# Filter rows in half transfers and a smaller fetch constant in the schedule: attention beside a long convolution on one core

## The chip, the cores and the metric

One core of a Trainium2 chip runs the whole program. The metric is device time in microseconds from launch to end; the time given for a kernel is the median of its runs. The engines named here are TensorE (PE, with its weight loads as PEld), VectorE (DVE), ScalarE (ACT), GpSimd (POOL) and SyncE (SP). Data move through 16 DMA engines, which serve several queues.

## The reference

Two independent blocks share the output, each 2048 x 512: multi-head attention with 32 heads of 16 columns (A), and a long convolution of 512 channels with gates (B). All inputs are bfloat16.

```python
def _A_ref(x, wqkv, wo):                       # x (1, 2048, 512), H = 32, Dh = 16
    q, k, v = split(x @ wqkv)
    scores = jnp.einsum("bhqd,bhkd->bhqk", q, k) * (Dh ** -0.5)
    p = softmax(scores)
    o = jnp.einsum("bhqk,bhkd->bhqd", p, v)
    return merge_heads(o) @ wo

def _B_ref(q, k, v, shift_k, ssm_k, ssm_D):    # each channel alone, over 2048 positions
    k_shift = 4-tap causal filter of k with shift_k
    kv = k_shift * v
    y = causal convolution of kv with ssm_k (2048 taps, by FFT of length 4096)
    y = y + kv * ssm_D
    return q * y

return jnp.concatenate([a, b], axis=-1)
```

## The kernel before

**Attention.** The scores are cut into 2048 blocks of 128 keys by 512 queries. For a step, `qk_mm` (L728) writes the scores of two or three blocks into PSUM banks, `emit_exp` takes the exponential of most of them in one ScalarE instruction (L761, with 512 columns for each block) and, where it can, gives one block to VectorE, which works out the exponential in four operations (`exp_on_dve`: L803, L810 twice, L815). Two steps later `emit_pv` (L844) multiplies the results with the values into another bank. After 64 blocks a head group is closed: a transpose (L905), a reciprocal and a product (L912, L916), and after two groups a second transpose (L925). Projections of queries, keys and values are done in pieces between the steps: a bank is lent for a few steps (a window, opened in `take_banks` when a job is due within OPEN steps), and `unit_step` puts the pieces into it; SLOT says how many steps a job is reckoned to need.

**Convolution.** For each channel the filter, reversed and padded, lies in HBM as a row of `kz_scratch`. A Toeplitz tile is read from it by one DMA with overlapping rows: partition p gets the 2048 values that begin at p, so 128 rows of 4 KB, 512 KB. Four channels make a quad (`qd`), and 128 quads make the 512 channels. `load_wr` (L990 to L997) issues the four DMAs of a quad on SP's queue as soon as one of four quad-sized places in `WR` is free; `conv_lags` (L1003 to L1033) multiplies for a range of lags, each lag with four matmuls (L1014), one for each channel, side by side in the array. A quad has 16 lags, so 64 matmuls, and the whole convolution 8192. After each four quads the result goes to SBUF (L1028), and after eight quads it is turned by eight transposes (L1039, `conv_turn`) and multiplied with the gate (L1048).

**The order.** The program is written out in full ahead of time, by a planner that runs while the kernel is built. It has a clock for each engine (class `Eng`), and `done` holds the planned end of each operation and transfer. `dma` plans a transfer: it begins when its engine and its inputs allow, lands `late` (4.2 us) later at the earliest, and the transfers follow one another at DMA_KB (394 KB/us). The class `Tensor` also follows TensorE's instruction fetch: every matmul counts as two instruction words, a block is BLOCK (256) words, and when one block is used up the next must have landed; the one after it is then planned to land FETCH later:

```python
            cross = self.t - (1.0 - part) * min(kw.get("run", 0.0), self.t - t0)
            stall = max(self.lands - cross, 0.0)
...
            self.lands = cross + stall + FETCH
```

`spare` tells how many words may still be used without running into that landing. Between the steps of the attention, `emit_bg` puts in a burst of lags. Its size is the least of LAGS, a budget that grows with time by PACE (and is set so that the convolution ends END steps before the PLAN of 710 steps), the time that is left before ScalarE needs its next scores, and what `spare` allows:

```python
        left_us = max(1.14 * (PLAN - END - T), 1.0)
        st["lags"] = min(st["lags"] + min(PACE * st["left"] / left_us, RATE) * (pe.t - st["t"]), CAP)
...
        left = min(LAGS, int(st["lags"]), int((room(T) - pe.turn("C") - SWITCH) / LAG), int(pe.spare() / 8))
        while left > 0 and st["qd"] < wr_next[0] and kv_n[st["qd"] // 32] == 4 and at(h_wr[st["qd"]]) + WAIT <= pe.t:
```

So a quad is begun only when its transfers are planned to have landed 1.5 us (WAIT) before. Where TensorE would be idle, `warm_up` puts in small matmuls on zeros (L1219). `dve_block` (L775 on) decides whether a step gives a block to VectorE: the step needs three banks, no lent bank that stands in the way, little enough planned work on VectorE, and enough blocks left, a limit into which TAIL_GAP enters. TURN says by how much `conv_turn` may make the next scores late.

Every engine then runs its list in order; waits are semaphores. What TensorE really waits for at run time is set by the chip and not by the plan.

Of the kernel before, what the change touches and what calls it, by code (L numbers as in the profile page):

```python
# [11 lines left out]
S = 2048  # L12
# [15 lines left out]
LEFT = 16  # L28
LKR = LEFT + S
R_W = 16  # L30
R_PT = 18
R_Q = 3
R_A = 4
# [1 line left out]
PVB = 6  # L35
BGB = 7
N_OPEN = 66
LAGS = 7
PACE = 1.4
KEYS0 = 256  # L40
END = 8

# [14 lines left out]
R_EH = 2  # L59
R_PTD = 5  # L60
T_DVE = 6
SLOT = 16
OPEN = 80
CLOSE = 12
REST = 2
LEN = 3
# [9 lines left out]
Q_DUE = 24  # L76
LOOK = 8
GAP = 7
TAIL_GAP = 4
AHEAD = 4  # L80
KZ_LATE = 8.0
KEEP = 4
# [3 lines left out]
DMA_KB = 394  # L86
X_KB = 200
WINDOW = 3.4
HALF = 0.25
TURN = 0.2  # L90
SOON = 0.5
NEAR = 0.2
FULL = 1.6
# [11 lines left out]
LAG = 0.0555  # L105
BLOCK = 256
WORD0 = 62
FETCH = 6.3
NEED = 10.0
FILL = 0.054  # L110

# [50 lines left out]
class Calls:  # L162
# [8 lines left out]
    transpose = matmul  # L171


class Tensor(Eng):
# [7 lines left out]
    def op(self, fn, deps=(), **kw):  # L182
# [6 lines left out]
        if words >= self.left:  # L189
# [3 lines left out]
            if stall:  # L193
                self.stalls.append((cross, stall))
                self.t += stall
                if kw.get("inc", True):
                    self.done[(id(self.sem), self.n)] += stall
            self.lands = cross + stall + FETCH
        self.at_word += words
# [20 lines left out]
def bass_concat_heads__mha_block__ssm_conv_h3__prompt_kernel(  # L220
# [13 lines left out]
    kz_ap = nc.dram_tensor("kz_scratch", (C, LKZ), BF16).ap()  # L234
# [7 lines left out]
    def sem(name):  # L242
        return enter(nc.semaphore(name))

    def sb(name, shape, dt=BF16):
        return enter(nc.sbuf_tensor(name, shape, dt))
# [6 lines left out]
    QS = sb("QS", [128, QB])  # L253
    PT = sb("PT", [128, R_PT, QB])
    WR = sb("WR", [128, R_W, S])
    WRF = WR[:, :, :].rearrange("p r w -> p (r w)")
# [25 lines left out]
    VST = [x.rearrange("p (t d) -> p t d", t=NB)  # L282
           for x in (WR[:, R_W - 2, :], WR[:, R_W - 1, :], OUTA[:, :, :].rearrange("p r d -> p (r d)"), VS2[:, :])]
    KZS = WRF[:, 0:4 * LKZ].rearrange("p (c m) -> p c m", c=4)
# [13 lines left out]
    act, dve, pool, sp = [Eng(sem(n), done) for n in ("s_act", "s_dve", "s_pool", "s_sp")]  # L298
    dma_t = [0.0]

    def at(*deps):
        return pe.at(deps)

    def dma(eng, dsem, outp, inp, deps=(), transpose=False, kb=512, rate=DMA_KB, late=4.2):
        h = dsem.add()
        start = max(eng.t, at(*deps))
        dma_t[0] = max(dma_t[0], start + late) + kb / rate
        done[(id(h[0]), h[1])] = dma_t[0]

        def fn(e):  # L310
            f = e.dma_start_transpose if transpose else e.dma_start
            f(outp, inp).then_inc(dsem.sem, 16)  # L312
        issue = kb / (rate if rate < DMA_KB else 155) if transpose else 0.55
        eng.op(fn, deps, inc=False, us=(issue, issue + 0.06))
        return h

# [37 lines left out]
    d_outA = [DmaSem(sem(f"d_outA{i}")) for i in range(R_A)]  # L354
    d_wr = [DmaSem(sem(f"d_wr{i}")) for i in range(R_W // 4)]

# [24 lines left out]
    for c in range(4):  # L381
        src = bass.AP(tensor=v2.tensor, offset=v2[128 * (NB - 1), 128 * c].offset, ap=[[D, 128], [-128 * D, NB], [1, 128]])
        h_vn.append(dma(sp, d_kv[3 + c], VST[c], src, kb=512))

    def load_kt(i, dep):
        h_kt[i] = dma(sp, d_kv[i], KTR[i][:, :, LEFT:LEFT + S], k2[:, (0, 256, 384)[i]:(256, 384, 512)[i]], [dep], transpose=True, kb=(1024, 512, 512)[i])
        h_kt0[i] = pool.op(lambda e: e.memset(KTR[i][:, :, 0:LEFT], 0.0), [dep])
# [102 lines left out]
    def evac_unit(u, bank, h):  # L490
# [18 lines left out]
        elif kind == "kv":  # L509
# [6 lines left out]
            if sum(kv_n[0:2]) == 8 and c < 2:  # L516
                load_qn(0, [h])
                wr_free.append((R_W // 4 - 1, hh))
                load_wr()
# [15 lines left out]
    h_kzw = [None]  # L535
# [15 lines left out]
    def kz_store(us):  # L551
# [3 lines left out]
        load_kt(2, h_kzt[0])  # L555
        wr_free.extend([(i, h_kzw[0]) for i in range(R_W // 4 - 1)])
        load_wr()
# [55 lines left out]
    def take_banks(T):  # L613
# [24 lines left out]
        else:  # L638
# [3 lines left out]
            banks = list(range(ends[1], 6))  # L642
        if T >= N_OPEN and near(T, OPEN) and T >= win.get("last", 0) + REST and "bank" not in win and len(banks) > 2 and late["bank"] is None and len(queue) > LAST_BLKS + 18:
            b = hold(T, banks, "w")
# [4 lines left out]
    def near(T, most):  # L649
        job = next_unit(T)  # L650
        return job is not None and job[0] - T <= most

    def hold(T, banks, kind):
        if T % 2 == 0:
            b = banks.pop()
            ends[0] -= 1
        else:
            b = banks.pop(0)
            ends[1] += 1
        held[b] = kind  # L660
        h_held[b] = T
        return b
# [3 lines left out]
    late = {"bank": None}  # L666
# [75 lines left out]
    def emit_exp(T, bl, banks, h, extra, d_bank, more):  # L742
        n = len(banks)
        if extra is not None:
            on_dve[extra] = len(on_dve)
            exp_on_dve(extra, d_bank, h)
        if pt_at[0] + n > R_PT:
            pt_at[0] = 0
# [22 lines left out]
    def pt_next():  # L771
        p = pt_at[0]
        return set(range(p, min(p + MOST, R_PT))) | (set(range(MOST)) if p + MOST > R_PT else set())

    def dve_block(T, bl):  # L775
        if len(bl) < 3 or WIN_D and "bank" in win and (part[0] or WIN_D > 1 and near(T, CLOSE)) or T < T_DVE or len(queue) < LAST_BLKS + 3 * (TAIL_GAP - N_LAST) + 3:
            return None
        i = len(on_dve)
        if i >= R_FX and i - R_FX not in h_last:
            return None  # L780
        todo = sum(us[0] for f in flow for _, _, _, us, _ in f)
        if max(dve.t - pe.t, 0.0) + todo > BACKLOG:
            return None
        n = blk_group(bl[-1])
        if len([b for b in queue if blk_group(b) == n]) - 3 >= 2.6 * GAP:
            return bl[-1]
        n += 1
        ahead = [b for b in queue if blk_group(b) == n]
        if len(ahead) < 4 * KT - AHEAD + 1 or n not in h_q or (OF[n], 0) not in h_k:
            return None  # L790
        rows = [blk(b)[2] for b in bl[:-1]]
        return next((b for b in ahead[:4] if blk(b)[2] not in rows), ahead[0])
# [4 lines left out]
    def exp_on_dve(b, bank, h):  # L797
        i = on_dve[b]
        fx = FX[:, i % R_FX, :]
        frac = fx.bitcast(U16).rearrange("p (n w) -> p n w", w=2)[:, :, 0]  # L800
        eh = EH[:, i % R_EH, :]
        out16 = PTD[:, i % R_PTD, :].bitcast(U16)
        h_f = urgent(lambda e: e.tensor_scalar(fx, PS[:, bank, :], FIX_ADD, FIX_HI, ALU.add, ALU.min),  # L803
                     [h, h_last.get(i - R_FX)], slack=S_FX)
        bank_free[bank] = h_f
        st = {"h": h_f}

        def square(j, us):
            src = frac if j == 0 else eh
            st["h"] = dve.op(lambda e: e.scalar_tensor_tensor(eh, src, (P1, P2)[j], src, ALU.add, ALU.mult),  # L810
                             [st["h"], h_last.get(i - R_EH)], us=us)

        def last(us):
            h_last[i] = h_blk[b] = dve.op(
                lambda e: e.scalar_tensor_tensor(out16, eh, P3, fx, ALU.mult, ALU.add),  # L815
                [st["h"], h_ptd.get(i - R_PTD)], us=us)
        dep = lambda: [st["h"]]
        flow.append([("p", dep, lambda us: square(0, us), V512,
                      lambda: i < R_EH or i - R_EH in h_last),
                     ("p", dep, lambda us: square(1, us), V512, lambda: True),  # L820
                     ("p", dep, last, V512, lambda: i < R_PTD or i - R_PTD in h_ptd)])
# [162 lines left out]
    h_wr, h_qn = {}, {}  # L984
# [5 lines left out]
    def load_wr():  # L990
        while wr_free and wr_next[0] < C // 4:
            (i, dep), qd = wr_free.pop(0), wr_next[0]
            wr_next[0] += 1
            wr_slot[qd] = i
            for c in range(4):
                src = bass.AP(tensor=kz_ap.tensor, offset=kz_ap[4 * qd + c, 0].offset, ap=[[1, 128], [1, S]])
                h_wr[qd] = dma(sp, d_wr[i], WR[:, 4 * i + c, :], src, [h_kzw[0], dep])  # L997

    def load_qn(i, deps):
        h_qn[i] = dma(pool, d_q[0], QN[:, :, :],  # L1000
                      q2[:, 256 * i:256 * i + 256].rearrange("(t p) d -> p t d", p=128), deps, kb=1860)
# [71 lines left out]
    def room(T):  # L1073
        lim = at(h_exp[min(T, end[0] - 1)]) - 0.47 - MARGIN
        return lim - max(pe.t, at(bank_free[BGB]))
# [8 lines left out]
    def press(T):  # L1084
        load = max([(i + 1) * SLOT / max(due - T, 1) for i, (due, u) in enumerate(jobs)], default=0.0)
        return SOON if load > FULL else NEAR if load > 0.75 * FULL else 0.0

    def unit_step(T):
# [7 lines left out]
        while not tight:  # L1096
# [16 lines left out]
            else:  # L1113
                ahead = (due - win["begin"] - 5) / SLOT
                over = TURN if u[0] == "turn" else 9.0 if ahead <= 1 else press(T)
                if T == stop - 1 and ahead > 2 and u[0] != "turn":
# [26 lines left out]
    def emit_bg(T):  # L1143
# [20 lines left out]
        if not st["started"]:  # L1164
            return
        left_us = max(1.14 * (PLAN - END - T), 1.0)
        st["lags"] = min(st["lags"] + min(PACE * st["left"] / left_us, RATE) * (pe.t - st["t"]), CAP)
        st["t"] = pe.t
        left = min(LAGS, int(st["lags"]), int((room(T) - pe.turn("C") - SWITCH) / LAG), int(pe.spare() / 8))
        while left > 0 and st["qd"] < wr_next[0] and kv_n[st["qd"] // 32] == 4 and at(h_wr[st["qd"]]) + WAIT <= pe.t:  # L1170
# [146 lines left out]
```

## Time and profile before

| | us |
|---|---|
| median of 3 runs (lowest, highest) | 827.02 (825.85, 828.55) |
| the profiled execution | 828.52 |
| its span, first to last instruction | 826.8 |
| granted TensorE clock in it, mean | 0.996 |
| PE idle before matmuls of L728 | 38.7 |
| last exponential ends | 819.7 |
| packet records: q1 packets of 4096 B | 65536, 0.159 each |

The span is what lies between the first and the last instruction of the profiled execution, and the 1.7 us more in its own time lie around it; that execution was 1.5 us over the median. Busy times of an engine are unions of its instructions, so mean durations times counts can come out higher: neighbouring instructions overlap. q1 is the hardware queue that carries the transfers issued by SP, and q8 carries instruction blocks; a packet record has its queue, start, duration and size. A line of the chain is start, duration and what it was; a line of a timeline is start, duration, engine, line, operation, tiles, count, and in brackets the idle time before it with what ended it.

The stages, from the table of windows (columns: window, its length, then busy time and instructions of PE, PEld, DVE, ACT, POOL, then the granted clock, the busy share of the DMA engines and GB/s):

```profile
40.00:100.00 60.00, 56.23 (x686) 24.96 (x690) 60.00 (x103) 59.68 (x53) 5.04 (x9) 1.00 0.76 251
100.00:200.00 100.00, 92.60 (x1858) 41.84 (x1857) 98.45 (x169) 99.41 (x91) 11.45 (x24) 1.00 1.02 389
200.00:300.00 100.00, 91.50 (x1778) 38.60 (x1784) 96.28 (x166) 96.84 (x86) 7.62 (x16) 0.98 1.03 399
...
700.00:800.00 100.00, 90.61 (x1686) 37.24 (x1689) 96.58 (x166) 97.44 (x87) 4.11 (x8) 0.98 0.90 341
800.00:827.00 27.00, 21.00 (x207) 7.08 (x206) 17.30 (x32) 20.79 (x20) 1.18 (x1) 1.00 0.20 59
```

The first score exponential starts at 7.9 us, the lags run from 89.5 to 804.1, and from 100 to 790 us the DMA engines are busy nearly all the time.

### The profile page before, as it was taken

To read this page: it belongs to the slowest core of one execution; us is meant where nothing else is said; L and a number is where in the kernel's file an instruction comes from. 1 tells how busy PE (TensorE), PEld (TensorE's weight loads), DVE (VectorE), ACT (ScalarE), POOL (GpSimd) and SP (SyncE) were. 2 spreads that over 40 slices of the span, in tenths; PEclk is the share of its full clock that TensorE was granted. 3 is DMA by queue.
4 is the path that set the end of the run, shared out by engine and by line. 5 is a ranking of instruction groups with operands and counts; after the bars stand their busy time and mean duration, and the time that the engine had idled before them with its cause. 6 is when DMAs were issued, how large, how long until landed. Compare 5 with 4: busy or idle time off the path is not lost.

```text
span 826.8 us, 30549 instructions
## 1 busy us (share of the span) xinstructions
PE 762.2 (92%) x13603; PEld 324.2 (39%) x13642; DVE 794.2 (96%) x1360; ACT 807.0 (98%) x727; POOL 78.7 (10%) x155
## 2 busy tenths in 40 slices
PE   8998989999999899999899999999999999998987
PEld 3343434443333344444333344444433333333332
DVE  4999999999999899999999999999999999999985
ACT  6999999999999899999999999999999999999987
POOL 3300320010100101001011010101002002010000
PEclk9999999999999999999999999999999999999999
DMA  9998499999999999999999899999999999999922
GB/s 220 233 300 304 151 382 404 385 379 407 393 407 405 394 401 389 405 354 367 394 388 391 318 372 383 394 408 387 408 407 352 378 393 362 399 382 367 375 83 77
DMA packets 109235, 291.41 MB, mean 352 GB/s; under 512 B 37680, under 2 KB 41648, under 8 KB 108720
## 3 DMA queue, kind: packets, MB, share of 16 engines
q1 hardware_dynamic: 102256, 280.80, 90.8%
q0 software_dynamic: 5648, 8.27, 3.1%
q8 instruction: 108, 1.77, 0.9%
q10 hardware_dynamic: 1200, 0.39, 0.2%
q14 instruction: 23, 0.19, 0.1%
HBM read 276.83 MB, written 6.42 MB: 343 GB/s over the span
## 4 chain that ended last, share of the span: by engine, by line
ACT 77%; DVE 10%; PE 9%; issue 2%; DMA 1%; SPq 0%
ACT PT L761 77%; DVE EH L810 4%; PE PS L728 3%; DVE FX L803 2%; PE PS L1014 2%; PE PS L844 2%; DVE PTD L815 2%; PE PS L1219 1%; PE PS L468 1%; DMA xT<-in_A_x_dram 1%; DVE DT L905 0%; DVE YB L1028 0%; SPq L312 0%; DVE KV L514 0%; DVE OTN L925 0%
## 5 line engine op out<-in xcount | busy, mean ns | idle before, releaser
L761 ACT ACTIVATE PT<-PS 128x1024 bf16<-128x1024 f32 (+2 forms) x722 | 804.1, 1376 | 8.8 <-PE PS L728 8.3
L728 PE MATMUL PS<-QT,KTo 32*128 32x512 bf16 x2048 | 287.1, 385 | 38.7 <-ACT PT L761 14.1
L844 PE MATMUL PS<-PT,VA 128*32 128x512 bf16 x1771 | 199.7, 391 | 6.6 <-issue 3.5
L1014 PE MATMUL PS<-WR,KV 128*12 128x128 bf16 (+15 forms) x8192 | 201.6, 220 | 4.4 <-issue 4.3
L803 DVE TENSOR_SCALAR FX<-PS 128x512 f32<-128x512 f32 x277 | 187.9, 682 | 8.3 <-PE PS L728 8.0
L815 DVE SCALAR_TENSOR_TENSOR PTD<-EH,FX 128x512 uint16<-128x512 f32 x277 | 185.7, 677 | 0.0
L810 DVE SCALAR_TENSOR_TENSOR EH<-EH 128x512 f32<-128x512 f32 x277 | 185.4, 680 | 0.0
L810 DVE SCALAR_TENSOR_TENSOR EH<-FX 128x512 f32<-128x512 uint16 x277 | 184.5, 682 | 0.1
L1014 PEld LDWEIGHTS PS<-WR,KV 128*12 128x12 bf16 (+15 forms) x8192 | 140.6, 88 | 71.9 <-issue 42.5
L728 PEld LDWEIGHTS PS<-QT,KTo 32*128 32x128 bf16 x2048 | 73.3, 91 | 237.8 <-ACT PT L761 178.9
L1219 PE MATMUL PS<-IDN,ZW 128*32 128x512 bf16 (+3 forms) x498 | 132.2, 334 | 0.0
L312 POOL DMA_DIRECT2D QT<-QS x120 | 59.2, 501 | 483.7 <-DVE DR L912 133.7
L844 PEld LDWEIGHTS PS<-PT,VA 128*32 128x32 bf16 x1771 | 48.0, 93 | 114.0 <-issue 97.5
L844 PE MATMUL PS<-PTD,VA 128*32 128x512 bf16 x277 | 83.1, 383 | 0.0
L1219 PEld LDWEIGHTS PS<-IDN,ZW 128*32 128x32 bf16 x498 | 41.8, 96 | 24.1 <-issue 10.4
L905 DVE STREAM_TRANSPOSE DT<-PS 128x512 f32<-128x512 f32 x32 | 22.7, 709 | 7.3 <-PE PS L844 6.8
L1028 DVE CAST YB<-PS 128x512 bf16<-128x512 f32 x32 | 21.9, 684 | 1.4 <-PE PS L1219 1.1
L844 PEld LDWEIGHTS PS<-PTD,VA 128*32 128x32 bf16 x277 | 20.4, 95 | 1.6 <-DVE PTD L815 0.2
L955 PE MATMUL PS<-WKV,OTN 128*128 128x512 bf16 x53 | 16.9, 383 | 2.1 <-issue 1.6
L479 PE MATMUL PS<-WKV,xT 128*128 128x128 bf16 x256 | 18.1, 220 | 0.1
L456 PE MATMUL PS<-xT,WKV 128*128 128x512 bf16 (+1 forms) x52 | 15.0, 373 | 2.9 <-issue 1.1
L447 PE MATMUL PS<-xT,WQ 128*128 128x512 bf16 x45 | 14.4, 382 | 2.4 <-issue 2.1
(65 smaller groups left out, 209.2 us busy)
## 6 DMA issues: line engine op xcount, KB each, us to landing
WR<-kz_scratch SPq DMA_DIRECT2D x512, 512.0 KB, 8.4
kz_scratch<-WR SPq DMA_DIRECT2D x1, 2176.0 KB, 8.3
QN<-in_B_q_dram POOLq DMA_DIRECT2D x2, 1024.0 KB, 12.4
out_dram<-QN POOLq DMA_DIRECT2D x2, 1024.0 KB, 8.6
QT<-QS POOLq DMA_DIRECT2D x120, 16.0 KB, 5.3
out_dram<-OUTA POOLq DMA_DIRECT2D x12, 128.0 KB, 5.2
QN<-in_B_ssm_k_dram SPq DMA_DIRECT2D x1, 1024.0 KB, 8.3
OTN<-in_B_ssm_k_dram SPq DMA_DIRECT2D x1, 1024.0 KB, 9.2
```

Source lines behind the costliest of these rows:

```text
L312: f(outp, inp).then_inc(dsem.sem, 16)
L479: ins = e.matmul(PS[:, bank, 128 * j:128 * j + 128], lhsT=xT[:, dc, (4 * sc + j) * 128:(4 * sc + j + 1) * 128], rhs=WV[:, dc, o * 128:(o + ...
L728: ins = e.matmul(PS[:, bank, :], lhsT=KTo[32 * s:32 * s + 32, OF[n_] % 2, kt * 128:(kt + 1) * 128], rhs=QT[32 * s:32 * s + 32, n_ // 2 % R ...
L761: h_exp[T] = act.op(lambda e: e.activation(PT[:, p0:p0 + n, :].rearrange("p b f -> p (b f)"), PS[:, banks[0]:banks[0] + n, :].rearrange("p ...
L803: h_f = urgent(lambda e: e.tensor_scalar(fx, PS[:, bank, :], FIX_ADD, FIX_HI, ALU.add, ALU.min), [h, h_last.get(i - R_FX)], slack=S_FX)
L810: st["h"] = dve.op(lambda e: e.scalar_tensor_tensor(eh, src, (P1, P2)[j], src, ALU.add, ALU.mult), [st["h"], h_last.get(i - R_EH)], us=us)
L815: lambda e: e.scalar_tensor_tensor(out16, eh, P3, fx, ALU.mult, ALU.add),
L844: ins = e.matmul(dst, lhsT=w, rhs=rhs, start=(k == 0), stop=(k == KT - 1), tile_position=(0, 32 * s))
L905: h_t = urgent(lambda e: e.transpose(out=dt, in_=PS[:, PVB, :]), [h, h_mul.get(n - 1)], slack=S_T, us=(0.63, 0.751))
L1014: ins = e.matmul(PS[32 * c:32 * c + NB - n, BGB, 128 * (kk % 4):128 * (kk % 4) + 128], lhsT=KV[:, qd, n:NB, c], rhs=WR[:, r + c, 128 * (NB ...
L1028: hh = urgent(lambda e: e.tensor_copy(YB[:, half, :].rearrange("p (k i) -> p k i", k=4), src), [h, h_yb[0]], slack=S_C, us=V512)
L1219: pe.op(lambda e, s=s, k=k, rhs=rhs, bank=bank, rows=rows, c0=c0, first=first: e.matmul(PS[32 * s:32 * s + rows, bank, c0:c0 + 128 * k], l ...
```

## The change

The 128 rows of a channel's Toeplitz tile are loaded by two DMAs of 64 rows each: partitions 0 to 63, then 64 to 127, on the same queue and with the same semaphore, so a quad has eight DMAs and not four. The planner is told of 256 KB for each and of 0.42 us for its issue (0.55 before). FETCH goes from 6.3 to 5.4. Seven other constants of the planner change with it: LAGS, PACE, END, SLOT, OPEN, TAIL_GAP and TURN. What is computed stays the same; where each instruction stands is worked out anew.

```diff
+WR_P = 64
...
-LAGS = 7
-PACE = 1.4
+LAGS = 6
+PACE = 1.2
 KEYS0 = 256
-END = 8
+END = 16
...
-SLOT = 16
-OPEN = 80
+SLOT = 18
+OPEN = 100
...
-TAIL_GAP = 4
+TAIL_GAP = 3
...
-TURN = 0.2
+TURN = 0.05
...
-FETCH = 6.3
+FETCH = 5.4
...
-    def dma(eng, dsem, outp, inp, deps=(), transpose=False, kb=512, rate=DMA_KB, late=4.2):
+    def dma(eng, dsem, outp, inp, deps=(), transpose=False, kb=512, rate=DMA_KB, late=4.2, issue=0.55):
...
-        issue = kb / (rate if rate < DMA_KB else 155) if transpose else 0.55
+        issue = kb / (rate if rate < DMA_KB else 155) if transpose else issue
...
             for c in range(4):
-                src = bass.AP(tensor=kz_ap.tensor, offset=kz_ap[4 * qd + c, 0].offset, ap=[[1, 128], [1, S]])
-                h_wr[qd] = dma(sp, d_wr[i], WR[:, 4 * i + c, :], src, [h_kzw[0], dep])
+                for p in range(0, 128, WR_P):
+                    src = bass.AP(tensor=kz_ap.tensor, offset=kz_ap[4 * qd + c, p].offset, ap=[[1, WR_P], [1, S]])
+                    h_wr[qd] = dma(sp, d_wr[i], WR[p:p + WR_P, 4 * i + c, :], src, [h_kzw[0], dep], kb=4 * WR_P, issue=0.42)
```

## The prediction

> **What bounds the kernel now.** I read the busy table first, then the chain that ended last, then the costliest groups, then timelines around ScalarE's idle moments, and last the packet records of the DMA queues.
>
> ```profile
> PE 762.2 (92%) x13603; PEld 324.2 (39%) x13642; DVE 794.2 (96%) x1360; ACT 807.0 (98%) x727; POOL 78.7 (10%) x155
> ...
> q1 hardware_dynamic: 102256, 280.80, 90.8%
> ...
> q8 instruction: 108, 1.77, 0.9%
> ...
> ACT 77%; DVE 10%; PE 9%; issue 2%; DMA 1%; SPq 0%
> ...
> L761 ACT ACTIVATE PT<-PS 128x1024 bf16<-128x1024 f32 (+2 forms) x722 | 804.1, 1376 | 8.8 <-PE PS L728 8.3
> L803 DVE TENSOR_SCALAR FX<-PS 128x512 f32<-128x512 f32 x277 | 187.9, 682 | 8.3 <-PE PS L728 8.0
> ...
> WR<-kz_scratch SPq DMA_DIRECT2D x512, 512.0 KB, 8.4
> ```
>
> ScalarE is the bound: 804.1 of 826.8 us go to the 722 exponentials of L761 (1771 score blocks; the other 277 go to VectorE, L803 to L815). Only what ends its idle time, or moves blocks to VectorE, can shorten the span. Before the last block (818.7 us) ScalarE loses 8.8 us, 8.3 of them to scores that come late (L728). The longer pieces of the chain say why:
>
> ```profile
> 105.01 1.13 issue
> ...
> 222.63 1.19 issue
> 229.25 0.72 issue
> ...
> 354.97 0.99 issue
> ...
> 787.25 1.98 issue
> ```
>
> "issue" is TensorE waiting for nothing that the profile shows. A sixth such stop, 1.57 us, is in the timeline at 278.4:
>
> ```profile
> 278.27 0.09 PEld L728 LDWEIGHTS PS<-QT,KTo 32*128 32x128 bf16 x1 [0.28 <-DVE FX L803]
> ...
> 279.93 0.09 PEld L728 LDWEIGHTS PS<-QT,KTo 32*128 32x128 bf16 x2 [1.57 <-issue]
> ...
> 280.37 1.45 ACT L761 ACTIVATE PT<-PS 128x1536 bf16<-128x1536 f32 x1 [0.87 <-PE PS L728]
> ```
>
> One score operation is cut after its first of three weight loads, so no semaphore holds it. Queue q8 holds the reason: its 108 packets are 16 KB each, about 256 TensorE instructions. In all six stops TensorE resumes 1.3 to 1.6 us after such a packet landed. ScalarE's idle moments behind the six are 0.42, 0.46, 0.62, 0.87, 0.58 and 2.13 us; the two longest stops are followed by a granted clock of 0.5 for 3.4 us (from 281.2 and 789.8), with 1.13, 0.25 and 0.18 us more. Sum: **6.64 us** of the 8.8 are instruction fetch; TensorE stood still 7.58 us for it.
>
> **What a fetch costs now.** After the four middle stops (222 to 356 us) packet records give a whole cycle: from resuming to the start of the next packet 3.75 to 4.23 us (median 3.9), the packet 1.08, landing to resuming 1.3 to 1.6: 6.2 to 6.9 us. Packets are 6.0 to 6.4 apart in 27 of 107 intervals, closer in 10. So the schedule's 6.3 is about the usual cost and leaves nothing for a long one. One stop differs: after 789.23 the next packet started in 1.81 us, when only the last filter transfers (landed by 792.0) were still in flight. That cycle is 1.81+0.93+1.42 = 4.2 us.
>
> **The change part by part.**
> (1) Halved transfers. A 4 KB row takes a DMA engine 159 ns (median of 65536). A 128-row transfer is 8 rows on each of 16 engines, 1.27 us; the half is 0.64. The 2.1 us that loaded traffic adds to a fetch (3.9-1.8) are 1.65 such turns. If a fetch waits for whole transfers, halves take 1.05 us off: cycle 5.3. Ends: 4.2 (all the waiting goes) and 6.3 (the wait goes by bytes). I take 5.3, as 1.65 turns is what waiting behind a transfer under way and one behind it would look like.
> The Trainium skill, "DMA: Bandwidth & Descriptors", section "Queues, rings and completion order", says that each engine goes round its queues by packets, groups of typically 9 to 17 descriptors. If a group ends with its transfer the cycle is 5.3, else 6.3; no row here shows the groups.
> (2) Issues. 512 more on SP at 433 ns (median): a quad of four channels takes 3.46 us of SP instead of 1.73. Quads land at least 5.1 us apart (2 MB), so SP keeps up; a median of 6 transfers is in flight at an issue. With that cover gone (at most one in flight at 7 of 512 issues), the last half starts 1.7 us later, against a median of 6.3 us from a quad's landing to its first use (least 0.2). Nothing queues behind these on SP until the final stores. Cost 0; at worst one wait of 1.5.
> (3) 8192 more completion writes at 9 ns (median of the 4-byte packets), over 16 engines: 4.6 us each, or 0.036 on the 5.1 of a quad. Landings run from 101.7 (fifth quad) to 792.0, 690 us for 123 intervals that need 627: 63 us of slack hide it. END 8 to 16 asks for the convolution 8 steps earlier, about 9 us, so transfers could slow by (63-9)/627 = 8.6% before they set the end. Cost 0.
> (4) FETCH 5.4, LAGS 6, PACE 1.2. Same 8192 matmuls in L1014, in bursts of at most 24, not 28 (the burst before 278.4 has 28, and so 56 instructions). Bursts of 7 need 293 groups, of 6 need 341; at twice the 0.105 us that the code's SWITCH allows for a change of kind, 10 us of TensorE, hidden in its 64.6 idle us; uncovered it would be 10 us. The fetch limit stands 0.1 above my cycle where it stood at or under it. The six stops should mostly go. Ends: none goes (0), all go (-6.6). I take 60%: **-4.0 us**, as the longest cycles lie 0.6 above the usual one and some will still overrun.
> (5) VectorE idles 9.9 us between 100 and 800, 7.3 of it at these stops. An operation there starts every 0.60 us, a block takes four, 2.4 us: three blocks would fit. A block off ScalarE saves about 0.45 (two-block exponentials start every 0.91). TAIL_GAP 3 allows one more; VectorE is idle 6.25 us before 820.2, so it is in time. SLOT, OPEN and TURN move when a bank is lent to projections; a step with two banks cannot give VectorE a block. Ends: +3 blocks, -3 blocks, 1.35 us each way. I take one more: **-0.4**.
> Sum -4.4 on a profiled execution of 828.5 (span 826.8 and 1.7 around it) gives 824.1. The median of the runs is 827.0, 1.5 lower, so I forecast **822.6**.
>
> **Rivals.**
> *Fetch does not shorten* (slower side). The wait goes by bytes, the cycle stays 6.3 and the schedule counts on 5.4. Place: wherever 256 instructions are packed into under 6.3 us, which 37 intervals nearly are now. 37 x 0.9 = 33 us of TensorE; today's six stops, with three of 0.76, 0.77 and 1.03 that cost nothing, pass on 6.64/10.1 = 0.65; about half the places remain with shorter bursts: +11, **838**. It decides once the real cycle exceeds some 5.7. For it: the packet itself takes 1.08 under load and 0.93 without, hardly a difference; against: 1.81 against 3.9 of waiting.
> *The schedule spends the gain.* The cycle falls, but bursts come closer and as many long fetches hit: **826.6**, only (5) remaining. For it: today's limit also matched the usual cycle, and six overruns remained.
> *Halves run one after another at half rate.* If 64 rows reach only half of what 128 do, a quad needs 10.2 us, and 101.7 + 123 x 10.2 + 35 (from the last landing to the end) gives about **1390**. Against it: rows of 159 ns x 32 on an engine are the 5.1 of a quad, so engines themselves are the limit now, and queued halves may overlap. It decides from 8.6%. The Trainium skill, "SBUF — State Buffer", section "Door 1: The DMA port swizzle (why `[64,N]` ≈ `[32,N]`)", says that partitions 0 to 63 reach 8 of 16 ports (196 against 328 GB/s at 1 MiB), and that two such transfers serialize. By that ratio a quad takes 8.5 us and the kernel, as an estimate, some 1180. No run here shows a large 64-row load.
> *Lent banks cost VectorE blocks.* OPEN 100 opens windows earlier; ten blocks fewer are 4.5 us: **831**. Against it: every job needs its window once in either schedule.
>
> **How the numbers follow.** Forecast 0.56, fetch not shorter 0.11, gain spent 0.18, half rate 0.06, fewer blocks 0.09. Runs of this kernel spread by 0.3% (825.85 to 828.55), so under 2.5 us is no change. Of the forecast nine tenths lie beyond -2.5 and the rest within; of "gain spent" 0.2 faster, 0.6 same, 0.2 slower; the others are slower. Faster 0.50+0.04 = 0.54, same 0.06+0.11 = 0.17, slower 0.29. The forecast's own range is 819 to 825.5. The range reaches down to 817 (all stops gone and three blocks) and up to 840, past fewer blocks and most of the unshortened fetch; outside it are the half rate and the tails, under 0.2.
>
> **What would show it.** Right: q8 packets as close as 5.2 to 5.4 us, resuming to next packet near 2.9; ScalarE's wait for L728 down from 8.3 to some 4; no second dip of the clock; 276 to 280 blocks in L803; 1024 WR issues with quads still 5.1 apart. Wrong: q8 packets never under 6 us and more "issue" pieces in the chain; quads over 5.5 us apart and L1014 waiting for DMA; fewer than 272 blocks in L803.

## The result

The changed kernel takes **1015.42 us** (median of 4 runs, 999.89 to 1030.38) against 827.78 (825.85 to 830.08) for the kernel before, measured beside it: a ratio of 1.2129, 95% interval 1.2025 to 1.2233. The forecast was 822.6 us, in a range of 817 to 840. The ratio goes by the two faster of the four runs (999.89 and 1008.36), because the other two count as the chip's slower state; with the median of all four it would be 1.227. The profiled execution took 999.89 us with a span of 998.1.

From the page of the changed kernel (lines moved down by one or two: the exponentials are L762, the scores L729, the lags L1016):

```profile
PE 823.1 (82%) x13668; PEld 343.7 (34%) x13708; DVE 803.7 (81%) x1360; ACT 823.1 (82%) x729; POOL 78.6 (8%) x155
...
GB/s 251 224 230 232 235 256 282 301 322 322 319 320 324 334 339 325 342 321 316 324 334 333 243 237 253 267 277 286 288 309 316 357 373 360 375 348 267 255 217 64
...
q1 hardware_dynamic: 110448, 280.83, 95.6%
...
DMA 40%; ACT 22%; PE 21%; SPq 13%; issue 3%; DVE 1%
...
L762 ACT ACTIVATE PT<-PS 128x1024 bf16<-128x1024 f32 (+2 forms) x724 | 820.2, 1259 | 163.5 <-PE PS L729 161.2
L1016 PE MATMUL PS<-WR,KV 128*14 128x128 bf16 (+15 forms) x8192 | 218.9, 233 | 131.7 <-DMA WR<-kz_scratch 123.7
...
L804 DVE TENSOR_SCALAR FX<-PS 128x512 f32<-128x512 f32 x277 | 189.2, 685 | 137.5 <-PE PS L729 137.1
...
WR<-kz_scratch SPq DMA_DIRECT2D x1024, 256.0 KB, 14.7
```

The lags in the kernel before:

```profile
L1014 PE MATMUL PS<-WR,KV 128*12 128x128 bf16 (+15 forms) x8192 | 201.6, 220 | 4.4 <-issue 4.3
```

The bound has moved. ScalarE was 98% busy, now 82%; its wait for scores went from 8.3 to 161.2 us, and behind that stands TensorE waiting at the lags for the filter loads, 123.7 us where the kernel before had none. The chain is now 40% filter loads. The DMA engines are busy throughout (q1 95.6%), but a busy engine moves less: a 4 KB row takes 208 ns at the median and 217 on average, against 159 and 169.5. The GB/s line, one figure for each 25 us, climbs and falls: 224 to 256 at first, some 320 from 200 us on, 243 again at 550, 375 later, and 267 at 900. The last filter row lands at 970.3 us (before 791.6). That is 178.7 us later, and the span is 171.3 longer. The granted TensorE clock is lower too, 0.922 on average against 0.996, and TensorE's busy time rises from 762 to 823 us; no run separates this from the waiting, but the late landings alone cover the longer span.

The chain in order of time shows the load stretches one after another, each the queueing and landing of one or more loads that TensorE needs before it goes on:

```profile
224.15 16.27 DMA WR<-kz_scratch
250.82 17.06 DMA WR<-kz_scratch
277.53 16.83 DMA WR<-kz_scratch
303.82 17.33 DMA WR<-kz_scratch
```

TensorE takes its list in order, so scores that are ready to be computed stand behind lags whose filter isn't there.

### The profile page after: what moved, and what is told of

Read it like the earlier page. It is cut to its first block, busy times and chain, and to the rows that moved or that the text cites. A ratio compares the mean times of both kernels' runs of the same rounds, so it can differ in the third digit from the quotient of the medians.

```text
span 998.1 us, 31204 instructions
## 1 busy us (share of the span) xinstructions
PE 823.1 (82%) x13668; PEld 343.7 (34%) x13708; DVE 803.7 (81%) x1360; ACT 823.1 (82%) x729; POOL 78.6 (8%) x155
## 3 DMA queue, kind: packets, MB, share of 16 engines
q1 hardware_dynamic: 110448, 280.83, 95.6%
## 4 chain that ended last, share of the span: by engine, by line
DMA 40%; ACT 22%; PE 21%; SPq 13%; issue 3%; DVE 1%
DMA WR<-kz_scratch 40%; ACT PT L762 22%; SPq L313 13%; PE PS L729 7%; PE PS L1016 5%; PE PS L845 4%; PE PS L1221 2%; PE PS L480 1%; PE PS L469 1%; DMA xT<-in_A_x_dram 0%; PE PS L956 0%; DVE EH L811 0%; PE PS L457 0%; DVE FX L804 0%; PE PS L590 0%
## 5 line engine op out<-in xcount | busy, mean ns | idle before, releaser
L762 ACT ACTIVATE PT<-PS 128x1024 bf16<-128x1024 f32 (+2 forms) x724 | 820.2, 1259 | 163.5 <-PE PS L729 161.2
L1016 PE MATMUL PS<-WR,KV 128*14 128x128 bf16 (+15 forms) x8192 | 218.9, 233 | 131.7 <-DMA WR<-kz_scratch 123.7
L729 PE MATMUL PS<-QT,KTo 32*128 32x512 bf16 x2048 | 306.8, 409 | 23.3 <-ACT PT L762 7.9
L1016 PEld LDWEIGHTS PS<-WR,KV 128*5 128x5 bf16 (+15 forms) x8192 | 146.1, 92 | 225.4 <-DMA WR<-kz_scratch 145.7
L845 PE MATMUL PS<-PT,VA 128*32 128x512 bf16 x1771 | 208.0, 411 | 4.1 <-issue 3.3
L1221 PE MATMUL PS<-IDN,ZW 128*32 128x512 bf16 (+4 forms) x563 | 159.8, 353 | 2.5 <-issue 1.9
L729 PEld LDWEIGHTS PS<-QT,KTo 32*128 32x128 bf16 x2048 | 73.2, 91 | 219.3 <-ACT PT L762 118.1
L845 PE MATMUL PS<-PTD,VA 128*32 128x512 bf16 x277 | 88.4, 406 | 0.0
L1221 PEld LDWEIGHTS PS<-IDN,ZW 128*32 128x32 bf16 (+1 forms) x563 | 51.1, 102 | 34.7 <-issue 19.5
L505 DVE CAST KTo<-PS 128x512 bf16<-128x512 f32 (+1 forms) x16 | 10.7, 671 | 10.4 <-PE PS L457 10.1
L527 DVE CAST VA<-PS 128x512 bf16<-128x512 f32 x16 | 11.0, 686 | 9.2 <-PE PS L480 9.1
```

What stands on the lines that cost most here:

```text
L729: ins = e.matmul(PS[:, bank, :], lhsT=KTo[32 * s:32 * s + 32, OF[n_] % 2, kt * 128:(kt + 1) * 128], rhs=QT[32 * s:32 * s + 32, n_ // 2 % R ...
L762: h_exp[T] = act.op(lambda e: e.activation(PT[:, p0:p0 + n, :].rearrange("p b f -> p (b f)"), PS[:, banks[0]:banks[0] + n, :].rearrange("p ...
L845: ins = e.matmul(dst, lhsT=w, rhs=rhs, start=(k == 0), stop=(k == KT - 1), tile_position=(0, 32 * s))
L1016: ins = e.matmul(PS[32 * c:32 * c + NB - n, BGB, 128 * (kk % 4):128 * (kk % 4) + 128], lhsT=KV[:, qd, n:NB, c], rhs=WR[:, r + c, 128 * (NB ...
L1221: pe.op(lambda e, s=s, k=k, rhs=rhs, bank=bank, rows=rows, c0=c0, first=first: e.matmul(PS[32 * s:32 * s + rows, bank, c0:c0 + 128 * k], l ...
```

## The experiments

Three theories: **half reach** (64 neighbouring partitions can be written at only half the rate of 128, as if the engines shared paths), **count** (each transfer has a price, and there are twice as many), and **schedule** (the new constants cost).

### The split without the constants

All eight constants of the changed kernel go back to what they were (the planner is still told of 256 KB and 0.42 us for each transfer):

```diff
-LAGS = 6
-PACE = 1.2
+LAGS = 7
+PACE = 1.4
...
-FETCH = 5.4
+FETCH = 6.3
```

> The changed kernel's two 64-row transfers with all eight constants as before (FETCH 6.3, LAGS 7 and so on). If the transfers themselves move slower (half reach or a price for each transfer), the time is near the changed kernel's, 970 to 1050 us, with TensorE waiting over 100 us for WR at the lags and the 4 KB rows at a median near 208 ns. If the new constants are what costs, it is near 828 us and the rows stay at 159 ns.

Measured: 1102.21 us in one run, above the range expected, and a median row of 246 ns. From its waits (engine, line and tile, who for, us in total, times, longest):

```profile
ACT PT L762 <- PE PS L729: 257.3, 200, 6.3
...
PE PS L1016 <- DMA WR<-kz_scratch: 192.0, 86, 6.1
```

So the split brings the loss without the constants, and more of it than with them.

### The constants without the split

```diff
-WR_P = 64
+WR_P = 128
...
-kb=4 * WR_P, issue=0.42)
+kb=4 * WR_P, issue=0.55)
```

> The eight constants of the change with whole 128-row transfers. If the split is the whole cost: no waiting for WR, rows at 159 ns, and the time is set by the fetch: with a real cycle of 6.2 us and more against the 5.4 that the schedule counts on, more and longer stops than before, 832 to 845 us (the forecast's rival had 838). If the constants carry the loss: over 950 us. If instruction fetch hardly matters: 824 to 830 us.

Measured: 823.87 us, ratio 0.9953 (0.9931 to 0.9975): below all three expectations, and faster than before.

```profile
ACT 94%; PE 3%; DVE 1%; DMA 1%; issue 1%; SPq 0%
...
L762 ACT ACTIVATE PT<-PS 128x1024 bf16<-128x1024 f32 (+2 forms) x724 | 802.9, 1382 | 3.0 <-PE PS L729 2.7
...
L1016 PE MATMUL PS<-WR,KV 128*14 128x128 bf16 (+15 forms) x8192 | 200.2, 220 | 1.8 <-issue 1.6
```

These are lines of its page. ScalarE's wait for scores is down from 8.3 to 2.7 us, and no stop for instruction fetch is long. Yet the fetch itself is no shorter: a tenth of the packets of the instruction queue follow within 6.05 us (before 6.01). So the constants gained by where the plan puts the work, not by a faster fetch; which of the moves did it isn't shown.

### Even and odd rows in place of lower and upper

```diff
-                for p in range(0, 128, WR_P):
-                    src = bass.AP(..., offset=kz_ap[4 * qd + c, p].offset, ap=[[1, WR_P], [1, S]])
-                    h_wr[qd] = dma(sp, d_wr[i], WR[p:p + WR_P, 4 * i + c, :], src, ...)
+                for p in range(128 // WR_P):
+                    step = 128 // WR_P
+                    src = bass.AP(..., offset=kz_ap[4 * qd + c, p].offset, ap=[[step, WR_P], [1, S]])
+                    h_wr[qd] = dma(sp, d_wr[i], WR[p:128:step, 4 * i + c, :], src, ...)
```

> The changed kernel, but the two transfers of a channel take the even and the odd rows in place of the lower and the upper 64: same number, size, queue and order of transfers, same constants. Half reach (64 neighbouring partitions reach half of what 128 do): rows back at about 160 ns, quads 5.1 us apart, no waiting for WR, 818 to 832 us, and then the fetch cycle shows whether a halved transfer shortens it (5.3 us if it waits for whole transfers, 6.2 if not). A price for each transfer, or for 64 rows as such: still near 1000 us with rows near 208 ns.

Measured: 844.64 us, ratio 1.0203 (1.0172 to 1.0234), some 13 us above the range expected for half reach. The rows are back at 159 ns. Number, size and order of the transfers are those of the changed kernel; only which partitions go together differs, and of its 21.3% of loss 2.0% are left. So half reach carries nine tenths of the loss. The schedule carries none of it with whole transfers (0.9953), and count at most what remains: 17 us over the kernel before, 21 over the same constants with whole transfers.

```profile
ACT 69%; DMA 11%; PE 10%; SPq 7%; issue 1%; DVE 1%
...
L762 ACT ACTIVATE PT<-PS 128x1024 bf16<-128x1024 f32 (+2 forms) x724 | 806.5, 1350 | 19.8 <-PE PS L729 18.8
L1017 PE MATMUL PS<-WR,KV 128*14 128x128 bf16 (+15 forms) x8192 | 200.5, 221 | 20.9 <-DMA WR<-kz_scratch 18.2
```

TensorE still waits 18.2 us for loads, and SP's queue is 7% of the chain. One issue on SP takes 597 ns at the median (433 for 128 rows), so eight take 4.8 us of a quad's 5.1, and all 1024 take 671 us (before, 512 took 250).

Two things differ from the constants with whole transfers. SP issues almost without pause: from the start of a quad's first issue to the end of its last it takes 5.54 us at the median (1.92 there), and between two of these issues it pauses for over 1 us only 5 times (122 times there). And some rows take longer: the mean is 172.4 ns against 168.4, which over the 4096 rows of an engine is 16 us. Which of the two sets the 21 us isn't shown.

### Loads alone

A kernel without the computation: five stages of 24 MB of loads on SP.

> Leaves out the whole computation and writes zeros: only loads of 24 MB on SP, 8 places deep, in five stages that wait for one another: whole 128-row transfers; 64-row transfers to partitions 0 to 63 only; lower and upper halves in turn; even and odd rows in turn; two column halves of 128 rows. Half reach: about 410 GB/s, 205, between 205 and 410 (starting low, as all engines begin on the same half), 410, about 400. A price for each transfer or for 64 rows: the second, third and fourth alike, near 290 to 320, the fifth no better.

From the table of windows, one window in the middle of each stage; the last column is GB/s, the one before it the busy share of the DMA engines:

```profile
10.00:60.00 50.00, 4.48 (x1) 1.00 0.99 404
80.00:180.00 100.00, 0.00 (x0) 1.00 1.03 208
200.00:290.00 90.00, 0.00 (x0) 1.00 1.04 235
310.00:360.00 50.00, 0.00 (x0) 1.00 1.01 408
380.00:430.00 50.00, 0.00 (x0) 1.00 1.03 385
```

Whole transfers 404, lower partitions only 208, halves in turn 235, even and odd rows 408, column halves 385 GB/s. Rows took 159, 320, 282 and 159 ns, and a 2 KB row 85. Engines are busy in all five; only in the two stages with 64 neighbouring partitions is each row slower, and twice as slow where the other half never comes. That is half reach, measured by itself. The source isn't the reason: the halves (235) and the even and odd rows (408) read the very same rows, and only the partitions that a transfer writes together differ. Alternating the halves helps by 13% here, no more. (Over whole stages, start and end included, the figures for whole transfers and column halves are 389 and 366, which the next forecast uses.)

### Column halves, and a schedule that knows the issue time

```diff
-                for p in range(0, 128, WR_P):
+                for m in range(0, S, S // 2):
...
-                    h_wr[qd] = dma(sp, d_wr[i], WR[p:p + WR_P, 4 * i + c, :], src, ...)
+                    h_wr[qd] = dma(sp, d_wr[i], WR[:, 4 * i + c, m:m + S // 2], src, ...)
```

> The changed kernel's constants and again eight transfers for a quad, but each takes all 128 rows and half of the columns (rows of 2 KB). Loads alone moved such halves at 366 GB/s against 389 for whole transfers, so 6% longer quads, 5.4 us, within the 8.6% of slack; an issue took 0.43 to 0.51 us, so 3.5 to 4.1 us of SP for a quad. Half reach: no big wait for WR, 820 to 835 us. A price for the number of transfers: near 1000 us.

Measured: 844.55 us, ratio 1.0198 (1.0173 to 1.0223): no 1000 us, but above what was expected.

```profile
ACT PT L762 <- PE PS L729: 20.0, 25, 3.9
PE PS L1016 <- DMA WR<-kz_scratch: 16.8, 16, 4.1
```

Its waits are those of the even and odd rows, with issues of 530 ns (628 us in all) and 2 KB rows of 86 ns, so 5.5 us for a quad.

The second edit is to the even and odd rows:

```diff
-kb=4 * WR_P, issue=0.42)
+kb=4 * WR_P, issue=0.6)
```

> Even and odd rows with the schedule told of 0.60 us for an issue (0.42 before), as the 64-row issues took 597 ns at the median. If SP's issue time is what kept the even and odd rows at 844 us (8 x 0.60 = 4.8 us of SP for a quad of 5.1), the schedule now takes the filters later and waits less for WR: 822 to 835 us. If the rows or the landings are slower for another reason, it stays at 842 to 848 us.

Measured: 844.77 us (ratio 1.0199, 1.0169 to 1.0228). Telling the schedule changed nothing. That SP's time is what is left is therefore not shown; that SP issues almost without pause would fit it, but no run shortened the issue. Both cuts that avoid half reach, even and odd rows and column halves, end at 844 to 845 us with eight transfers for a quad.

### FETCH by itself

The kernel before with one constant changed, and the constants without the split with FETCH at other values:

> The kernel before with FETCH 5.4 alone. If a schedule that counts on a fetch of 5.4 runs into one of 6.2, as the forecast's rival had it: 832 to 845 us, with more and longer pieces of issue in the chain. If the fetch limit hardly binds: 824 to 830 us.

> Whole transfers, the seven other constants of the change, but FETCH back at 6.3. If the seven constants bring the gain of 0.47% that the eight brought together, 821 to 825.5 us. If FETCH 5.4 brings it, 826 to 830 us, as before.

> Whole transfers, the seven other constants of the change, FETCH 5.6. If the gain at 5.4 belongs to the constants as such, within 2 us of 823.9. If the schedule answers any small edit with stops in other places, between 822 and 835 us without order, as 6.3 gave 828.1.

> The same with FETCH 5.2. If the gain at 5.4 belongs to the constants as such, within 2 us of 823.9. If a fetch that is counted on too short costs in proportion, 1 to 3 us over it. If the schedule answers any small edit with stops in other places, between 822 and 835 us without order.

| constants | FETCH | us | ratio (95%) | ScalarE's wait for scores, us |
|---|---|---|---|---|
| before | 6.3 | 827.8 (829.2 beside the runs at 6.3 and of the line below, 828.1 beside 5.6 and 5.2) | 1 | 8.3 |
| before | 5.4 | 839.08 | 1.0134 (1.0100 to 1.0168) | 15.1 |
| of the change | 6.3 | 828.12 | 0.9987 (0.9958 to 1.0016) | 7.8 |
| of the change | 5.6 | 827.35 | 0.9987 (0.9963 to 1.0010) | 7.5 |
| of the change | 5.4 | 823.87 | 0.9953 (0.9931 to 0.9975) | 2.7 |
| of the change | 5.2 | 821.01 | 0.9920 (0.9892 to 0.9949) | 2.2 |

The ratios are those on record, which are not always the quotients of the two medians: by these, the second line is 1.012. The waits are those of one execution each.

From the waits of the kernel before with FETCH 5.4:

```profile
ACT PT L761 <- PE PS L728: 15.1, 22, 2.5
PE PS L1014 <- issue: 10.3, 10, 2.5
```

TensorE's stops at the lags grew from 4.3 to 10.3 us, ScalarE's wait with them: the forecast's rival, where it was to be. With the seven other constants the same 5.4 costs nothing: the ratios are alike at 6.3 and 5.6 and fall at 5.4 and 5.2, to 821.01 us, the fastest kernel of this study, some 7 us under the kernel before (828.13 beside it). Its page:

```profile
L762 ACT ACTIVATE PT<-PS 128x1024 bf16<-128x1024 f32 (+2 forms) x724 | 802.9, 1370 | 2.4 <-PE PS L729 2.2
```

Why the two sets of constants answer in opposite ways isn't settled; the packets are no closer together in either (a tenth within 6.05 to 6.16 us at 5.4 and 5.2).

### Why the rate climbs

Halves in turn moved 235 GB/s alone, but up to 375 (all queues together) in the changed kernel. Four more kernels without the computation looked for the reason.

> Leaves out the whole computation and writes zeros: only lower and upper halves in turn on SP, five stages of 80 half transfers, each but the first begun with one extra load. Theory of the lead: engine e and engine e+8 share one path in either half, and share it for as long as both work on the same half; an engine that is ahead stays ahead by the same amount. An extra load of 8 rows goes to engines 0 to 7 alone and holds them up: 8 KB rows by half of a half transfer's time on an engine (0.64 us), 16 KB by the whole, 32 KB by twice. Rows then take about 280 ns without it (as the loads alone had), 200 to 250 with 8 KB, 159 to 200 with 16 KB, near 280 again with 32 KB, and near 280 with 16 rows of 16 KB, which go to all engines alike. Rival, a 64-row transfer is slow in itself, whatever the engines' order: near 280 in all five stages.

> Leaves out the whole computation and writes zeros: lower and upper halves in turn on SP, first 80 pairs with nothing beside them, then 160 pairs while TensorE works through 5000 small matmuls, whose instructions are fetched in 16 KB packets by the same DMA engines. If other packets that hold up single engines shift the engines out of step, rows start near 285 ns in the second stage too and fall toward 200 within some 100 us, as in the changed kernel (288 to 207 ns between 90 and 190 us), the rate rising from 233 to about 300 GB/s. If the rise in the changed kernel has another cause (gaps in its queue, other transfers), rows stay near 285 ns in both stages.

> Leaves out the whole computation and writes zeros: lower and upper halves in turn on SP, five stages of 48 pairs that wait for one another: 4 pairs in flight at most; 16 pairs; 16 pairs, issued four pairs at a time once their four places are free (as the kernel issues a quad); 8 pairs, four at a time; 8 pairs beside 64 loads of 16 rows of 1 KB on GpSimd's queue (as the kernel's QT). Theory of the depth: the more halves are queued, the further engines can get out of step; rows near 290 ns with 4 pairs and toward 200 with 16. Theory of the bursts: only the stages issued four at a time leave 285 ns. Theory of the other queue: only the last stage does. If all five stay at 280 to 295 ns, none of the three makes the changed kernel's rows faster than those of the loads alone.

> Leaves out the whole computation and writes zeros: lower and upper halves in turn on SP in three stages: 60 pairs whose source begins 4096 bytes further with each channel, as in the earlier loads alone; 100 pairs with 4352 bytes, the pitch of the kernel's scratch rows; 120 pairs with 4352 bytes beside 3600 matmuls whose instructions are fetched. If the source's pitch makes engines drift apart, rows fall from about 285 toward 200 ns in the second stage; if pitch and fetch together do, in the third alone. If all three stay at 280 to 295 ns, the climb in the changed kernel has another cause.

Median row of each stage, in ns, and GB/s from its first to its last row:

```
loads_lead   no lead 293, 231   8 KB 288, 233   16 KB 285, 235   32 KB 287, 228   all engines 291, 229
loads_fetch  alone 279 to 282, 236   with instruction fetch 273 to 293, 230 to 243
loads_depth  4 pairs 291, 233   16 pairs 284, 236   bursts, 16 292, 234   bursts, 8 284, 236   other queue 281, 224
loads_pitch  4096 B 293, 233   4352 B 282, 239   4352 B with fetch 282, 237
```

All stay at 273 to 293 ns (medians of 20 us in the second kernel): neither an extra load on eight engines, nor instruction fetch, depth, bursts, small transfers on another queue or the source's pitch makes rows fall toward 200 ns. One thing in the changed kernel points to engines that get out of step with time: the only moment after 50 us at which no filter row moved for more than 0.2 us is at 566.8 us, and the median row goes from 188 ns (550 to 570 us) to 281 (570 to 590) across it. But the fall of the rate at 900 us has no such moment. Both falls do come when little is queued: from 105 us until the last loads, the changed kernel has fewer than 7 half transfers issued and not begun only at 552 to 578 us and at 890 to 903. Whether that is what brings the rate down isn't tested, and what lifts it stays open.

## Why the prediction was wrong, point by point

**The failed step is part (3)**, which put the halved transfers at "Cost 0" by counting only their completion writes (0.036 us on a quad) and kept the 5.1 us between quads. A row went from 169.5 to 217 ns on average. Scaled by that, the 690 us of landings become 883, and 101.7 + 883 = 985 us; the last row landed at 970.3. So slower rows account for the difference. The same assumption is in part (1), where half a transfer is put at 0.64 us. The threshold of part (3), 8.6%, was passed at once: 28%.

**The rival "halves run one after another at half rate"** had the mechanism, with 0.06. The argument against it, that "engines themselves are the limit now, and queued halves may overlap", took the 159 ns of a row for a property of the engine; loads to the lower half alone show 320 ns on the same engines. Its price of 1390 was too high, since rows were slowed to 217 ns on average and not to 320: 1015. The rule of the Trainium skill cited there ("SBUF — State Buffer", section "Door 1: The DMA port swizzle (why `[64,N]` ≈ `[32,N]`)") agrees with the loads alone: 208 against 404 GB/s is its half. That two such transfers serialize stands on the same page of the Trainium skill, but in its section "Can I just issue two DMAs to hit both halves?"; here two halves in turn gained 13%. The estimate by its figures, 1180, is too high here as well; what the changed kernel reached in its faster stretches, 300 to 375 GB/s, neither that page of the Trainium skill nor any run of loads alone shows.

**Part (1), a fetch cycle of 5.3**: where rows run at full rate (even and odd rows), a tenth of the packets from 89.5 us on, when the lags run, follow within 5.32 us, and 27 of 101 under 6 (before: 6.01 us and 10 of 101; with 0.60 us planned for an issue: 5.68 and 22 of 101). The number was met in the first of these, its reason not shown: column halves hold an engine for 8 x 86 = 0.69 us, much like 4 x 159 = 0.64, and a tenth of their packets follow only within 6.19. Either rows count and not time, or the even and odd rows' queue is thinner because SP fills it more slowly. In the changed kernel no packet of that stretch follows within 6.6 us; slower rows make the fetch longer, as the loads with fetch beside them show (some 8.6 us at rows of 282 ns). The one cycle without load was 4.1 us rather than 4.2, as its packet took 0.88 us and not 0.93; nothing hangs on it.

**Part (2), issues**: 433 ns was taken for a half transfer too; it is 597, so 4.8 us of a quad's 5.1 and not 3.46, and 5.54 with the longer issues among them. That was no cost at all in the sum; an upper bound for it is the 20.8 us between even and odd rows (844.64) and the constants with whole transfers (823.87).

**Part (4)**: -4.0 us for the six stops. The constants with whole transfers are 3.9 us faster than before, by ScalarE's wait for scores going from 8.3 to 2.7. So the size was met by luck: it came with an unchanged fetch, against the reason given, and with the same constants FETCH 6.3 gains nothing. The rival "fetch does not shorten", 838 us, is what FETCH 5.4 does to the kernel before (839.08), and not what it does with the other constants.

**Part (5)**: one more block for VectorE was forecast; it is 277 in both kernels.

## What to carry to other kernels

Before a load is cut along partitions, ask which partitions go together: with the engines busy all the time, cut by even and odd rows or along the row if it must be cut at all (both still cost 2% here), and cost a transfer by the time of its rows with those partitions, not by bytes or by the rows of the whole transfer. A rule that speaks against a change and has no counterexample in the trace deserves more than 0.06 when the resource it names is busy for nine tenths of the span. Test the constants of a schedule without the edit that they came with: here they gain 0.5% by themselves and 0.8% with FETCH 5.2, while with the edit the kernel is 21% slower.

## What the runs showed of the hardware that was not expected

- Loads to partitions 0 to 63 alone take 320 ns for each 4 KB row with the engines busy throughout; 64 even and 64 odd partitions in turn take 159, as 128 do.
- Halves in turn are hardly better than the lower half alone (235 against 208 GB/s), in all 16 such stages of loads alone between 224 and 239.
- Issuing a 64-row load on SP takes longer than a 128-row one: 597 against 433 ns in the kernels, 465 (halves) and 595 (even and odd) against 328 in the first loads alone.
- Instruction fetch gets slower with the loads beside it: cycles of 6.0 to 6.4 us at rows of 159 ns, 8.2 to 9.0 at rows of 282 with 16 half transfers queued.
